# A new order for the instruction list of a fused attention and gated-MLP block

## The chip, the cores and the metric

The kernel runs on one core of one Trainium2 chip. The core has five engines that run on their own instruction streams: TensorE (PE, matrix products), VectorE (DVE), ScalarE (ACT), GpSimd (POOL) and SyncE (SP, which here issues DMAs). They wait for one another by semaphores. The metric is the device time of one execution in microseconds, as the median of three runs.

## The reference

One sequence of 2048 tokens with 448 features goes through two blocks whose normalized inputs are modulated by a conditioning vector `c`:

```
mod = silu(c) @ w_mod                      # six vectors: sa, ca, ga, sb, cb, gb
h = layernorm(x) * (1 + ca) + sa
q, k, v = split(h @ wqkv)                  # 16 heads of 28
p = softmax(q k^T / sqrt(28), masked to the last 256 positions)
x = x + ga * ((p v) @ wo)
h = layernorm(x) * (1 + cb) + sb
z = gelu(h @ w_in)                         # 1792 columns: z1 and z2, 896 each
g = w_sp @ layernorm(z2) + b_sp            # w_sp is 2048 x 2048
out = x + gb * ((z1 * g) @ w_out)
```

All data are bfloat16; products accumulate in float32.

## The kernel before

The tokens are cut into 16 tiles of 128, and four of these make a block `tb`. The program first collects a list of operations. Each has a number, the engines that could do it with a planned duration for each ("ways"), the operations it depends on, and the buffers it takes ("Hold", "Res"). Nothing in that list sets the order. The order is a text, `ORDER`: each entry is the number of an operation, one letter for the engine that does it (p TensorE, a ScalarE, v VectorE, g GpSimd, s SyncE), and the index of the buffer it takes. `Sched.order` reads the entries one after the other and appends each operation to its engine's stream; an engine does its stream strictly in that order. Buffers are given in list order too, so that who waits for whom over a buffer also follows from the list. `Sched.waits` then puts in the semaphore waits that the dependences need. The planned durations in the code only sort the waits of an instruction; they decide no order once `ORDER` stands.

The stages, with the lines that the prediction speaks of:

- The start. `w_mod`, `wqkv` and the first tokens are loaded. Statistics of a tile are taken on VectorE (L605, L608), then come the variance plus epsilon (L610, VectorE or GpSimd), its power of -1/2 (L613, GpSimd only), the negative scaled mean (L617 on VectorE, L620 on GpSimd), and the normalized tile (L625 on VectorE, L627 on ScalarE, L630 on GpSimd). Tiles are turned on TensorE (L692) and scaled into `hT` (L699, L701). The weights for q and k are copied into padded form `WQK` (L596, L597), and GpSimd and ScalarE clear `QBD` (L530, L531). Warm-up products (L561) keep TensorE running.
- Attention, for each tile and each half of the heads: scores into four PSUM banks (L952) and one bank more (L961), exponentials on ScalarE (L913), masks on VectorE (L968), the products with the values (L995). There is one set of four banks for the scores, so a new L952 can't begin before the exponential of the last one is read. Between these run the q, k and v projections of later blocks (L782, L811, L824) with their evictions (L792, L816, L817, L828, L829), the division (L1009, L1011), the output projection (L1019), the residual sum (L1024) and the second layer norm with the copy of its last columns (L633, L634). SyncE turns tiles by DMA; the result is scaled with the modulation (L682, L684 for the first norm, L1042 and L1044 for the second).
- The gated MLP. The z2 half (L1081, GELU L1092 and L1104 on ScalarE, squares L1113, small operations L1108, normalization L1096 on GpSimd, L1099 and L1118 on VectorE) and the z1 half (L1127, GELU L1135) are both products with half of TensorE's rows, written by the helper at L855 in groups of four steps that take two pairs of banks.
- The spatial products (L1151): 28 groups of 16 matmuls with 512 columns, which need all normalized z2 tiles and the transposed `w_sp` (wspA for the first two blocks, wspB for the others). VectorE adds the bias (L1155), GpSimd multiplies by z1 (L1158), TensorE makes the output product (L1170), VectorE adds the residual (L1181), SyncE stores.

## Time and profile before

| | us |
|---|---|
| three runs, median (lowest to highest) | 278.40 (278.39 to 279.79) |
| the profiled execution, its own time | 277.81 |
| its span, first to last instruction | 276.1 |
| TensorE busy with matmuls | 265.1 |
| VectorE busy | 161.2 |
| ScalarE busy | 134.8 |
| GpSimd busy | 124.2 |

The granted clock of TensorE is 1.0 throughout. "Busy" is the time in which an engine has an instruction under way; a matmul's end is modelled, so that a busy TensorE may still have waited a little. The span is about 1.7 us shorter than the profiled execution's time, since the time also holds what lies before the first and behind the last instruction. In a row of a group, the number after the bar is the busy time in all, then the mean duration of one in ns, then the idle time of the engine just before them with what ended it. In a row of the timeline stand the start and the duration in us. In a row of the stretches stand first the stretch, its length and the busy time of PE, PEld (weight loads), DVE, ACT and POOL with the number of instructions.

### The profile page before, as it was taken

The numbers are of one execution on the slowest core, as the hardware profiler recorded it, in microseconds if no ns is written. First come the engines' busy times: TensorE is split into PE (matmuls) and PEld (weight loads), VectorE is DVE, ScalarE is ACT, GpSimd is POOL, SyncE is SP. The second block draws the span as 40 slices with busy tenths as digits, with TensorE's granted clock in tenths as the row PEclk, the third lists the DMA queues.
The fourth block names the chain that finished last, engine by engine and source line by source line (L and its number), as shares of the span: only waits on it lengthen the run. The fifth ranks groups of instructions, "written<-read, shape, count | busy, mean of one in ns | idle before, by whom it ended". The sixth has DMA issues, their size and how long they took to land.

```text
span 276.1 us, 7474 instructions
## 1 busy us (share of the span) xinstructions
PE 265.1 (96%) x3230; PEld 142.0 (51%) x3230; DVE 161.2 (58%) x364; ACT 134.8 (49%) x185; POOL 124.2 (45%) x182
## 2 busy tenths in 40 slices
PE   5699999999999999999999799999999999999995
PEld 3465565557577565445444344444444444444453
DVE  6888998989899999985548101025040221322453
ACT  4589998899999998559997400000000000000000
POOL 7830528635107695786499300028370311543310
PEclk9999999999999999999999999999999999999999
DMA  7946955262333748545999999200000000001023
GB/s 216 304 167 198 255 104 106 41 96 60 69 71 57 106 67 172 104 92 103 184 183 212 161 203 190 49 0 0 0 4 0 0 17 2 0 17 33 19 86 97
DMA packets 67595, 26.54 MB, mean 96 GB/s; under 512 B 58021, under 2 KB 66474, under 8 KB 67562
## 3 DMA queue, kind: packets, MB, share of 16 engines
q1 hardware_dynamic: 67288, 25.61, 45.0%
q8 instruction: 25, 0.41, 0.6%
q10 hardware_dynamic: 274, 0.46, 0.5%
q14 instruction: 8, 0.07, 0.1%
HBM read 9.53 MB, written 1.84 MB: 41 GB/s over the span
## 4 chain that ended last, share of the span: by engine, by line
PE 77%; DVE 15%; ACT 2%; DMA 2%; issue 1%; POOL 1%; ACTq 0%; DVEq 0%
PE ps L1151 35%; PE ps L1081 8%; PE ps L1127 8%; PE ps L1170 8%; DVE PT L968 6%; PE ps L782 5%; PE ps L995 3%; PE ps L824 3%; PE ps L1019 3%; PE ps L952 2%; DMA wmod<-in_w_mod_dram 2%; DVE o_sb L1011 1%; DVE st_all L605 1%; DVE x_sb L1024 1%; POOL rs_all L613 1%
## 5 line engine op out<-in xcount | busy, mean ns | idle before, releaser
L913 ACT ACTIVATE PW<-ps 128x2048 bf16<-128x2048 f32 (+1 forms) x56 | 68.0, 1244 | 3.7 <-PE ps L952 2.1
L1155 DVE TENSOR_TENSOR tmpg<-ps,bsp_bc 128x512 bf16<-128x512 f32 x28 | 19.0, 690 | 80.9 <-PE ps L1151 66.4
L1158 POOL TENSOR_TENSOR z1T<-tmpg,z1T 128x512 bf16<-128x512 bf16 x28 | 31.7, 1152 | 76.1 <-DVE tmpg L1155 76.1
L1151 PE MATMUL ps<-wspA,z 128*128 128x512 bf16 x224 | 48.5, 380 | 1.7 <-ACT z1T L1135 1.7
L1151 PE MATMUL ps<-wspB,z 128*128 128x512 bf16 x224 | 49.2, 380 | 0.0
L968 DVE TENSOR_TENSOR PT<-PW,mask 128x1024 bf16<-128x1024 bf16 x56 | 37.9, 708 | 0.2 <-ACT PW L913 0.2
L1151 PEld LDWEIGHTS ps<-wspA,z 128*128 128x128 bf16 x224 | 21.8, 98 | 28.4 <-POOL z L1096 2.1
L1151 PEld LDWEIGHTS ps<-wspB,z 128*128 128x128 bf16 x224 | 21.9, 98 | 26.3
L613 POOL TENSOR_TENSOR rs_all<-ve_all,neghalf 128x1 f32<-128x1 f32 (+1 forms) x31 | 21.8, 710 | 14.3 <-DVE ve_all L610 13.2
L995 PE MATMUL ps<-Vaug,PT 128*128 128x32 bf16 x496 | 24.5, 177 | 0.8 <-DVE PT L968 0.4
L995 PEld LDWEIGHTS ps<-Vaug,PT 128*128 128x128 bf16 x496 | 21.5, 96 | 4.3 <-DVE PT L968 1.0
L1127 PE MATMUL ps<-hT,w_in 64*128 64x512 bf16 x196 | 22.1, 377 | 0.0
L1081 PE MATMUL ps<-w_in,hT 64*128 64x448 bf16 x224 | 22.1, 350 | 0.0
L1170 PE MATMUL ps<-w_out_g,z1T 128*128 128x448 bf16 (+2 forms) x126 | 22.0, 332 | 0.0
L995 PE MATMUL ps<-Vaug,PW 128*128 128x32 bf16 x224 | 20.4, 177 | 0.0
L782 PE MATMUL ps<-hT,WQK 128*128 128x512 bf16 x80 | 19.6, 380 | 0.1
L605 DVE BATCH_NORM_STATS2 st_all<-x_sb 128x6 f32<-128x448 bf16 x32 | 19.1, 610 | 0.1
L995 PEld LDWEIGHTS ps<-Vaug,PW 128*128 128x128 bf16 x224 | 17.7, 96 | 1.9
L1170 PEld LDWEIGHTS ps<-w_out_g,z1T 128*128 128x128 bf16 x126 | 11.7, 98 | 10.1
L630 POOL TENSOR_SCALAR xn<-x_sb,rs_all,ve_all 128x448 bf16<-128x448 bf16 x17 | 16.0, 944 | 1.1 <-DVE ve_all L617 0.5
L1135 ACT ACTIVATE z1T<-ps 128x512 bf16<-128x512 f32 x28 | 14.6, 604 | 3.4 <-PE ps L1127 3.3
L1081 PEld LDWEIGHTS ps<-w_in,hT 64*128 64x128 bf16 x224 | 10.8, 94 | 10.5 <-DVE mv_all L1108 0.3
(122 smaller groups left out, 356.0 us busy)
## 6 DMA issues: line engine op xcount, KB each, us to landing
out_dram<-fin SPq DMA_DIRECT2D x15, 112.0 KB, 1.7
x_sb<-in_A_x_dram SPq DMA_DIRECT2D x3, 448.0 KB, 4.5
wmod<-in_w_mod_dram SPq DMA_DIRECT2D x1, 1344.0 KB, 8.3
w_in<-in_B_w_in_dram SPq DMA_DIRECT2D x1, 1344.0 KB, 7.4
QBD<-qT SPq DMA_DIRECT2D x16, 64.0 KB, 2.1
w_out_g<-in_B_w_out_dram SPq DMA_DIRECT2D x1, 784.0 KB, 5.9
bsp_bc<-in_B_b_sp_dram SPq DMA_DIRECT2D x1, 512.0 KB, 5.2
x_sb<-in_A_x_dram SPq DMA_DIRECT2D x2, 224.0 KB, 3.6
```

The costliest lines, as they stand in the source:

```text
L605: st = [dve(0.62 if True else 0, lambda e, t=t, ci=ci, s=s: e.bn_stats(st_all[:, slot, t, ci, :], s()), deps(t), prio) for ci, s in enumer ...
L613: rs = pool(0.41 + 0.155 * len(tiles), lambda e: e.tensor_tensor(rs_all[:, slot, a:b], ve_all[:, slot, a:b], neghalf[:, 0:b - a], ALU.pow) ...
L782: m = pe(4 * MMS, [lambda e, h=h, g=g, kc=kc, tb=tb: e.matmul(ps[:, h.slot[0], :], lhsT=WQK[:, kc, 4 * g:4 * g + 4, :].rearrange("p a b -> ...
L913: ex = act(xdur, lambda e, out_ap=out_ap, in_ap=in_ap: e.activation(out_ap(), in_ap(), ACT.Exp, scale=SCALE), [s], v - 8.0 + u, takes, tab ...
L968: return dve(0.68, lambda e: e.tensor_tensor(cols(hp.slot[0] * 2048 + 1024 * k, [[256, 4], [128, 2], [1, 128]]), cols(at_w() + 128 + 192 * ...
L995: fns.append(lambda e, hp=hp, hO=hO, hi=hi, bi=bi, kb=kb, hd=hd, nb=nb, a=at[hi][bi], p_of=p_of: e.matmul(ps[:, hO.slot[0], 32 * hd:32 * h ...
L1081: return lambda e, kc, p0, start, stop: e.matmul(ps[:, hs[t % 2].slot[hf], 0:D], lhsT=hT[p0:p0 + 64, kc, t * 128:(t + 1) * 128], rhs=w_in[ ...
L1127: return lambda e, kc, p0, start, stop: e.matmul(ps[:, hs[b // 2].slot[b % 2], :], lhsT=w_in[p0:p0 + 64, kc, ft * 128:(ft + 1) * 128], rhs ...
L1151: m = pe(16 * MMS, [lambda e, h=h, si=si, ft=ft, tb=tb: e.matmul(ps[:, h.slot[0], :], lhsT=z2[:, si, ft * 128:(ft + 1) * 128], rhs=(wspA i ...
L1155: a = dve(0.7, lambda e, h=h, ht=ht, tb=tb: e.tensor_tensor(tmpg[:, ht.slot[0], :], ps[:, h.slot[0], :], bsp_bc[:, tb * 512:(tb + 1) * 512 ...
L1158: u = pool(1.16, lambda e, ht=ht, ft=ft, tb=tb: e.tensor_tensor(z1T[tb][:, ft, :], tmpg[:, ht.slot[0], :], z1T[tb][:, ft, :], ALU.mult), [ ...
L1170: return [lambda e, ft=ft: e.matmul(ps[:, h.slot[0], c0:c1], lhsT=z1T[t // 4][:, ft, (t % 4) * 128:(t % 4 + 1) * 128], rhs=w_out_g[:, ft, ...
```

## The change

The text `ORDER` is replaced by another with the same operations, two further warm-up products (76 and 77) aside. Nearly every entry stands in another place. 107 operations change engines as well: for instance, thirteen of the L617/L620 operations move from GpSimd to VectorE and three the other way, six normalized tiles move from GpSimd to VectorE and two the other way (L625, L630), and ScalarE has six hT scalings of the second norm (L1042) where it had one. In the code, four planned durations of GpSimd operations are raised; the instructions themselves stay as they are. An excerpt of the list, and all edits of the code:

```diff
@@ ORDER, the start @@
-2.a 25.v 35.g 0.s 26.v 27.v 28.v 38.g 39.g 3.a 4.s 36.g 45.a 33.g 29.v 5.s 30.v 31.v 37.g 32.v 40.g 6.s 7.s 41.g 138.v 139.v 140.v 141.g 46.p.0 48.a
...
-112.v 163.v 164.v 165.p.3 131.a 132.g 130.g 49.g 73.p.6 74.p.7 75.p.0 174.p.4.5 175.p.6.7 176.p 166.a 177.p 178.p 179.p 167.a 8.s 1.s 133.a 182.p
-180.p 183.p 181.p 150.v 151.v 152.g 153.g 9.s 10.s 11.s 134.a 188.p.0.1 189.p.2.3 14.s 13.s 12.s 16.s 15.s 156.v 157.v 158.v 159.g 154.v 136.v 155.v.2
-137.g 187.a 184.a 186.a 160.v 161.v.3 135.v 171.p.7 172.a 173.a 168.p.4 190.p 191.p 192.p 193.p 195.p 194.p 197.p 196.p 169.v 170.v 230.v 232.v
...
-224.p.6 213.p.7 210.p.0 383.a.0 388.p.0 217.a 225.a 389.a.1 228.p.7 214.a 229.a 34.g 52.g 51.g 239.g 42.g 223.v 240.v 243.v.0 244.g.1 44.g 43.g
...
+2.a 25.v 35.g 0.s 26.v 27.v 28.v 38.g 39.g 3.a 4.s 36.g 45.a 33.g 29.v 5.s 30.v 31.v 37.g 32.v 40.g 6.s 7.s 41.g 46.p.0 48.a 47.a 144.v 8.s 145.v 1.s
...
+14.s 71.p.0 72.p.3 165.p.2 112.v 111.v 162.p.3 12.s 131.v 130.a 166.v 133.g 163.v 16.s 167.a 73.p.6 74.p.7 75.p.0 76.p.6 174.p.4.5 150.v 164.a 13.s
+175.p.6.7 50.a 77.p.0 176.p 151.v 15.s 156.v 177.p 152.g 178.p 153.g 179.p 135.a 157.v 183.p 181.p 158.v 134.v 180.p 159.g 154.v 187.a 188.p.0.1 185.v
+189.p.2.3 155.a.2 136.g 190.p 160.v 191.p 161.v.3 42.g 168.p.7 171.p.5 137.g 192.p 169.v 193.p 49.g 194.p 172.v 182.p 170.a 197.p 195.p 196.p 173.v
+198.a 43.g 234.v 199.a 204.p.7 51.g 184.a 232.v 203.p.5 200.a 186.a 205.p.0 235.v 201.a 236.v 52.g 207.a 202.p.1 208.a 230.v 382.p.0 209.a 224.p.6
...
@@ ORDER, the end of attention @@
-817.p.0 818.p 772.p.1 820.a.3.2 822.a 823.v 824.v 847.a 547.g.0 849.g 548.g 744.v 773.v 687.v 518.g.2 825.p 850.g 826.p 914.p.0 519.g 827.v 828.v.0
-915.p.1 916.p 896.p.3 897.p.2 898.p 917.p 899.p 918.a 632.g 660.g 661.g 633.g 381.s 549.s 520.s 800.s 829.s 688.v 689.g 634.g.1 662.g 845.g 745.v
...
+546.v 716.v 800.s 817.p.0 547.g.1 772.p.1 577.g 548.v 744.v 822.a 896.p.0 823.v 897.p.1 816.v 578.s 773.v 898.p 824.v 818.p 825.p 549.s 717.v 629.v
...
@@ ORDER, the hand-over to the spatial products @@
-846.g 1032.a.1 945.a.0 999.g 1006.v 946.v 1033.g 913.v 1034.g 992.g 993.g 1027.v 1028.g 947.g 1000.v 1014.v 1007.v 1008.v 907.g 959.v 1035.v 977.g
...
-1053.p.0 1054.p 1085.p.3 1055.p 1086.p 1087.p 1009.g 1010.g 1011.g 994.v 1016.g 930.v 1017.g 1012.g 948.v 924.v 863.s 1057.a 1056.a 1091.a 1058.a
-1090.a 1059.a 1088.a 1089.a 894.s 895.s 882.s 886.s 887.s 890.s 893.s 891.s 892.s 880.s 883.s 1029.v 1018.v 1140.p.4 1110.p.5 1134.p.6 1135.v.0
...
+1085.p.3 1029.v 890.s 1064.a 1011.v 1012.g 1086.p 1065.a 1087.p 880.s 942.g 1052.p.2 1091.a 907.g 1090.a 1053.p.0 882.s 1054.p 977.g 881.s 1055.p
+845.g 1110.p.6 1059.a 883.s 840.g 1058.a 1057.a 1088.a 893.s 1089.a 1056.a 1140.p.7 894.s 886.s 887.s 1107.p.0 891.s 863.s 892.s 1104.p.1 884.s 895.s
...
@@ costs of GpSimd operations @@
-        ways = {"pool": (0.23, lambda e: e.tensor_scalar(ve_all[:, slot, a:b], mv_all[:, slot, a:b, 1], EPS, None, ALU.add))}
+        ways = {"pool": (0.31, lambda e: e.tensor_scalar(ve_all[:, slot, a:b], mv_all[:, slot, a:b, 1], EPS, None, ALU.add))}
-        return [rs, add({"dve": (0.16, by), "pool": (0.27, lambda e: e.tensor_scalar(ve_all[:, slot, a:b], mv_all[:, slot, a:b, 0], rs_all[:, slot, a:b], -1.0, ALU.mult, ALU.mult))}, [rs], prio)]
+        return [rs, add({"dve": (0.16, by), "pool": (0.33, lambda e: e.tensor_scalar(ve_all[:, slot, a:b], mv_all[:, slot, a:b, 0], rs_all[:, slot, a:b], -1.0, ALU.mult, ALU.mult))}, [rs], prio)]
-                         "pool": (0.25, lambda e: e.tensor_copy(to[:, h.slot[0], D:DP], to[:, h.slot[0], DP - 128:D]))}, [op], prio)]
+                         "pool": (0.28, lambda e: e.tensor_copy(to[:, h.slot[0], D:DP], to[:, h.slot[0], DP - 128:D]))}, [op], prio)]
-                return add({"dve": (0.13, fn), "pool": (0.2, fn)}, deps, v)
+                return add({"dve": (0.13, fn), "pool": (0.29, fn)}, deps, v)

```

## The prediction

> **What bounds the kernel now.** I read the page's head first, then the busy time of each engine in stretches cut at the first exponential, the last exponential and the two ends of the gated MLP. The columns behind each stretch are its length, then the busy time of TensorE's matmuls, its weight loads, VectorE, ScalarE and GpSimd.

> ```profile
> span 276.1 us, 7474 instructions
> ...
> 0.00:18.75 18.75, 13.72 (x129) 8.74 (x130) 14.86 (x44) 11.63 (x26) 12.35 (x26) 1.00 0.81 243
> ...
> 24.00:107.40 83.40, 82.09 (x1993) 52.32 (x1990) 79.17 (x173) 79.41 (x83) 41.62 (x54) 1.00 0.53 98
> ...
> 109.20:153.50 44.30, 44.28 (x430) 20.90 (x428) 31.25 (x89) 33.74 (x63) 33.22 (x66) 1.00 0.83 152
> 153.50:155.20 1.70, 0.04 (x1) 0.07 (x2) 1.29 (x1) 1.68 (x4) 1.16 (x2) 1.00 1.18 57
> 155.20:273.20 118.00, 118.00 (x574) 55.34 (x574) 28.19 (x44) 1.37 (x3) 32.66 (x29) 1.00 0.20 46
> ```

> From 155.2 to 273.2 TensorE never stops (118.00 of 118.00), and from 109.2 to 153.5 it has 0.02 us idle: no order can shorten these two stretches, since the change adds and removes no matmul there. What is left is the start (18.75 us to the first exponential), the attention stretch, where ScalarE is idle for 83.40 - 79.41 = 4.0 us and VectorE for 4.2 us, and one hole of 1.7 us at 153.5. That is all a new order can win; it can lose without such a bound, in the attention stretch above all.

> **The change part by part.** Comparing the two lists entry by entry: both hold the same operations but for two more warm-up matmuls (76 and 77) at the start. Every engine's order changes. VectorE goes from 364 to 380 entries, GpSimd from 178 to 157, ScalarE from 168 to 173. The four raised GpSimd costs change no instruction; they only move the planned times.

> *The start.* These are VectorE's, GpSimd's and ScalarE's instructions there (start, duration).

> ```profile
> 7.69 0.86 DVE L701 TENSOR_SCALAR hT<-ps,modT 128x256 bf16<-128x256 bf16 x2 [0.45 <-PE ps L692]
> ...
> 10.50 0.27 DVE L596 COPY WQK<-wq_st 128x448 bf16<-128x448 bf16 x1
> 10.69 0.38 DVE L625 TENSOR_SCALAR xn<-x_sb,mv_all,rs_all 128x448 bf16<-128x448 bf16 x1
> 11.54 1.17 DVE L625 TENSOR_SCALAR xn<-x_sb,mv_all,rs_all 128x448 bf16<-128x448 bf16 x1
> 12.63 1.10 DVE L596 COPY WQK<-wq_st 128x448 bf16<-128x448 bf16 x1
> ...
> 10.88 0.61 POOL L597 COPY WQK<-wq_st 128x448 bf16<-128x448 bf16 x1
> 11.63 1.97 POOL L531 MEMSET QBD<- 128x1024 f32 x2
> ...
> 7.74 0.58 ACT L596 ACTIVATE WQK<-wq_st 128x448 bf16<-128x448 bf16 x1 [1.29 <-DMA wq_st<-in_A_wqkv_dram]
> 18.75 1.02 ACT L913 ACTIVATE PT<-ps 128x1024 bf16<-128x1024 f32 x1
> ```

> The same normalization takes 0.38 us at 10.69 and 1.17 at 11.54, the same copy 0.27 at 10.50 and 1.10 at 12.63; during the long ones GpSimd clears QBD (two memsets, 1.97 us). Both long ones stand on the way to the first exponential: 0.79 + 0.83 = 1.6 us. The new list puts these copies (134, 135, 136) ahead of the normalization, gives tile 2's normalization (155) to ScalarE, and moves the two memsets (51, 52) behind. Two things take some of it back. The weight copy 131 moves from ScalarE to VectorE ahead of the two L701, and its data comes only at 7.74, so those start 7.74 + 0.27 - 7.69 = 0.3 us late, and tile 2's statistics behind them. And GpSimd still runs a 0.61 us copy (136) where normalization 161 comes, which can hold it for up to that. I take -1.0 us; the ends are -1.6 (nothing given back) and 0 (all of it, by a chain now hidden).

> [...]

> *The attention stretch.* Rows by group within 24.0 to 107.4 (count | busy us, mean ns), one instruction from the timeline, two waits; the second L968 row is of 70 to 80 us, where GpSimd does nothing (count: shortest/median/longest).

> ```profile
> L816 ACT ACTIVATE KT<-ps 128x512 bf16<-128x512 f32 x1 | 0.6, 592 | 0.0
> L767 ACT ACTIVATE KT<-ps 128x256 bf16<-128x256 f32 x1 | 0.4, 378 | 0.0
> ...
> 107.42 0.80 ACT L1042 ACTIVATE hT<-hT,modT 128x512 bf16<-128x512 bf16 x1
> ...
> ACT PW L913 <- PE ps L952: 2.1, 7, 0.5
> ...
> L968 DVE TENSOR_TENSOR PT<-PW,mask 128x1024 bf16<-128x1024 bf16 x54 | 36.7, 709 | 0.2 <-ACT PW L913 0.2
> L605 DVE BATCH_NORM_STATS2 st_all<-x_sb 128x6 f32<-128x448 bf16 x18 | 10.8, 610 | 0.0
> ...
> L1024 DVE TENSOR_TENSOR x_sb<-ps,x_sb 128x448 bf16<-128x448 f32 x12 | 7.4, 617 | 0.7 <-PE ps L1019 0.6
> ...
> L817 DVE CAST KT<-ps 128x512 bf16<-128x512 f32 x3 | 2.0, 675 | 0.0
> L617 DVE SCALAR_TENSOR_TENSOR ve_all<-mv_all,rs_all 128x4 f32<-128x4 f32 (+1 forms) x4 | 1.5, 377 | 0.8 <-POOL rs_all L613 0.7
> L625 DVE TENSOR_SCALAR xn<-x_sb,mv_all,rs_all 128x448 bf16<-128x448 bf16 x3 | 1.4, 471 | 0.0
> ...
> L684 DVE TENSOR_SCALAR hT<-hT,modT 128x512 bf16<-128x512 bf16 x3 | 1.1, 394 | 0.0
> L574 DVE COPY gg_sb<-ps 128x448 f32<-128x448 f32 x1 | 0.6, 619 | 0.0
> ...
> L968 DVE TENSOR_TENSOR PT<-PW,mask x5: 659/684/687, 74.0 to 77.6; 128x1024 bf16<-128x1024 bf16 x5
> ...
> L630 POOL TENSOR_SCALAR xn<-x_sb,rs_all,ve_all 128x448 bf16<-128x448 bf16 x13 | 13.0, 1003 | 0.7 <-DVE ve_all L617 0.3
> ...
> L620 POOL TENSOR_SCALAR ve_all<-mv_all,rs_all 128x1 f32<-128x1 f32 x6 | 3.7, 623 | 0.5
> ...
> DVE ve_all L617 <- POOL rs_all L613: 1.7, 4, 0.7
> ```

> ScalarE, between its first and its last exponential: two more K evictions (L816, 2 x 0.59), one more hT scaling (0.80), the gate copy from VectorE (L574; 0.62, no ScalarE row, bounds 0.38 and 0.80 from its other copies), two L767 fewer (2 x 0.38). Sum +1.8 us on an engine with 4.0 us idle, of which 2.1 us are waits for the scores (L952).

> VectorE, between its first and last mask: statistics 13 to 9 (-4 x 0.61), L817 three to one (-2 x 0.68), residual sums 12 to 14 (+2 x 0.62), norms +3 x 0.47, hT scalings +2 x 0.39, L617 +3 x 0.38; the others cancel. Sum: -2.44 - 1.35 + 1.23 + 1.41 + 0.79 + 1.13 = +0.8 us.

> GpSimd up to the last mask: four L620 fewer (-4 x 0.62) and one L630 (-1.0); the rest, scalings and small copies that come and go, stays within 0.4 us: about -3.5 of 41.6 us. A mask takes 709 ns on average against 684 with GpSimd silent: 54 x 0.025 = 1.35 us lost to it in the stretch, of which 3.5/41.6 is 0.1 us. That relief is small.

> TensorE: three of the four steps of the first MLP group (896 to 898, L855) move ahead of the last three attention products. That work fills the wait for the last exponentials, and TensorE's idle in the stretch is 83.40 - 82.09 = 1.3 us.

> So the stretch gets +1.8 us on ScalarE, and must eat 1.8 of its 4.0 us idle to stay as long. Ends: +1.8 (idle unchanged) and -2.2 (no idle left). The list cannot tell which; I take the middle, 0. GpSimd's work moved onto VectorE is hidden only while VectorE keeps its remaining idle of 4.2 - 0.8 = 3.4 us.

> *After attention.* ScalarE gets four more hT scalings (4 x 0.80 = 3.2 us) between 107 and 153, where it is idle 44.30 - 33.74 = 10.6 us: hidden. Then the hole:

> ```profile
> 153.53 3.04 ACT L1135 ACTIVATE z1T<-ps 128x512 bf16<-128x512 f32 x6 [1.72 <-PE ps L1127]
> 153.57 1.09 POOL L1096 TENSOR_SCALAR z<-z,rs_all,ve_all 128x896 bf16<-128x896 bf16 x1
> ...
> 155.16 2.10 PE L1151 MATMUL ps<-wspA,z 128*128 128x512 bf16 x9 [1.68 <-ACT z1T L1135]
> ```

> The first spatial product waits for a free bank (ScalarE's GELU) and for the last normalized tile (GpSimd, done at 154.66). In the new list it takes a bank of the group before the last (1110 in bank 6, freed by GELU 1090), so the first cause goes. Next late is GpSimd, whose four normalizations (1012, 942, 907, 977) now come in a row, the last beside TensorE's last two steps. I take -1.0; ends -1.7 and +0.5 (half a normalization more than now).

> *The last stretch.* Its order changes most, but only a stall could cost.

> ```profile
> L1155 DVE TENSOR_TENSOR tmpg<-ps,bsp_bc 128x512 bf16<-128x512 f32 x28 | 19.0, 690 | 80.9 <-PE ps L1151 66.4
> L1158 POOL TENSOR_TENSOR z1T<-tmpg,z1T 128x512 bf16<-128x512 bf16 x28 | 31.7, 1152 | 76.1 <-DVE tmpg L1155 76.1
> L1151 PE MATMUL ps<-wspA,z 128*128 128x512 bf16 x224 | 48.5, 380 | 1.7 <-ACT z1T L1135 1.7
> ...
> L1170 PE MATMUL ps<-w_out_g,z1T 128*128 128x448 bf16 (+2 forms) x126 | 22.0, 332 | 0.0
> ...
> bsp_bc<-in_B_b_sp_dram SPq DMA_DIRECT2D x1, 512.0 KB, 5.2
> ...
> 148.50 24.03 SPq L477 DMA_TRANSPOSE wspB<-in_B_w_sp_dram  x16
> ```

> On SyncE the bias load moves behind 13 of the 16 wspB transposes: 148.5 + 13 x 1.50 + 5.2 = 173. A group takes 16 x 48.5/224 = 3.46 us and there are eight banks, so the ninth needs one at 155.2 + 27.7 = 182.9: hidden by 10 us, minus one eviction. At the end two output groups (2 x 7 x 22.0/126 = 2.4 us) instead of four cover the last L1155 and L1158 (0.69 + 1.15 = 1.84 us): hidden, with 0.6 us to spare. Term 0.

> Sum: -1.0 + 0 - 1.0 + 0 = -2.0 us. The profiled execution took 277.81 us, so 275.8; the median of the runs, 278.40, lies 0.6 above it, so **276.4** is what I predict for the median.

> **The rivals.** *A, VectorE stuck behind GpSimd (slower).* L617 on VectorE waits for GpSimd's power (L613), and all queued behind it, masks included, waits too. Up to the last mask there are 12 such entries instead of 8 and 11 norms on VectorE instead of 9. At the longest wait (0.7) and the longest hold (1.17 - 0.38), 4 x 0.7 + 2 x 0.79 = 4.4 us: 276.4 + 4.4 = 280.8. It makes the kernel slower by over 0.5% from 3.4 us up. For it: VectorE has only 4.2 us idle in 83. Against: four such waits are 1.7 us now, and most moved entries come late. *B, ScalarE's stream is the wall (no change).* Its idle stays: +1.8, so 278.2. For it: the waits for scores are a turn-around through one set of banks (L952 writes where the exponential before reads), which an order hardly shortens. Against: it has 4.0 us. *C, all holes close (faster).* -1.6, -1.3 (TensorE's attention idle), -1.7: 4.6 us, 273.8. [...]

> **How the numbers follow.** Half a per cent, 1.4 us, is about what a measurement of this kernel can tell from no change. My forecast 0.41, C 0.12: faster 0.53. B 0.22: same. A 0.25: slower. The range reaches to A's and C's prices: 273.5 to 281.0; the forecast's own is 274.5 to 277.8.

> **What would show it.** Start: the first exponential at about 17.7, no L625 or L596 over 0.7 us before it. Attention: first to last exponential still 89 us; ScalarE's waits for L952 under 2.1 us. Hole: first L1151 within 0.7 us of the last L1127. End: matmuls back to back for 118 us. I am wrong if VectorE's waits for L613 grow past 3 us, if a mask waits behind them, or if the stretch between the exponentials grows by more than 2 us.

## The result and the profile after

The new list takes 275.25 us (median; 274.60 to 276.79), the old one beside it 278.72 us (278.08 to 279.79): a ratio of 0.9874, with an interval of [0.984, 0.9908], that is 3.5 us or 1.3% less. The profiled execution of the new kernel took 275.39 us with a span of 273.7; that of the old one had 277.81 and 276.1. So the pair of profiles that is compared below holds 2.4 of the 3.5 us; the other 1.1 us is what these two executions differ from the medians by. Here and below a median is of all executions, while a ratio is taken on those within 1.5% of the fastest of their kernel, without two of e3 and three of e4, and is no quotient of medians.

The columns of the next fence are those of the prediction's stretches: length, then busy time of TensorE, weight loads, VectorE, ScalarE and GpSimd. It is the new kernel, cut at the first exponential, the last exponential and the first spatial product, and at the last stretch.

```profile
0.00:19.81 19.81, 15.83 (x133) 9.97 (x134) 13.75 (x45) 10.99 (x25) 13.21 (x30) 1.00 0.75 230
...
152.74:270.74 118.00, 118.00 (x574) 55.49 (x574) 27.99 (x44) 3.04 (x6) 36.75 (x33) 1.00 0.25 49
...
19.81:107.65 87.84, 87.22 (x2068) 56.11 (x2068) 82.04 (x189) 85.75 (x92) 30.47 (x45) 1.00 0.52 103
107.65:152.74 45.09, 45.09 (x461) 21.46 (x457) 31.34 (x102) 38.11 (x68) 25.80 (x55) 1.00 0.83 155
```

The same two middle stretches of the old kernel, from the last exponential on up to its first spatial product:

```profile
18.75:107.52 88.77, 87.36 (x2071) 55.74 (x2070) 83.52 (x184) 84.75 (x91) 43.35 (x59) 1.00 0.53 102
107.52:155.16 47.64, 45.96 (x466) 22.14 (x463) 34.22 (x92) 37.04 (x68) 35.81 (x69) 1.00 0.85 153
```

Stage by stage, in us (the first exponential stands for its start, the last for its end):

| stage | old | new | difference | predicted |
|---|---|---|---|---|
| start, to the first exponential | 18.75 | 19.81 | +1.06 | -1.0 |
| attention, first to last exponential | 88.77 | 87.84 | -0.93 | 0 |
| hand-over, last exponential to first spatial product | 47.64 | 45.09 | -2.55 | -1.0 |
| the rest | 120.92 | 120.94 | +0.02 | 0 |

In attention ScalarE works 1.0 us more (84.75 to 85.75) and is idle 1.9 us less (88.77 - 84.75 = 4.02 us before, 87.84 - 85.75 = 2.09 after). In the hand-over TensorE had 47.64 - 45.96 = 1.68 us idle and now has none; besides it has 0.87 us less to do there (45.96 to 45.09): four matmuls of the output projection (L1019, 8 in this stretch instead of 12) and the first 0.57 us of the gated MLP (L1081, begun at 107.08) now run before the last exponential ends at 107.65. How the hole closed stands in the timeline of the new kernel (start, duration):

```profile
149.45 3.23 POOL L1096 TENSOR_SCALAR z<-z,rs_all,ve_all 128x896 bf16<-128x896 bf16 x3
...
149.76 2.97 PE L1127 MATMUL ps<-hT,w_in 64*128 64x512 bf16 x26
...
152.74 4.49 PE L1151 MATMUL ps<-wspA,z 128*128 128x512 bf16 x20
```

GpSimd's normalizations end at 152.68, the last L1127 at 152.73, and the first spatial product begins at 152.74. In the old kernel the last GpSimd normalization ran from 153.57 to 154.66.

### The profile page after: what moved, and what is told of

The parts are those of the page before. It is cut to its first block, busy times and chain, and to the rows that moved or that the text cites. A ratio compares the mean times of both kernels' runs of the same rounds, so it can differ in the third digit from the quotient of the medians.

```text
span 273.7 us, 7480 instructions
## 1 busy us (share of the span) xinstructions
PE 266.2 (97%) x3232; PEld 143.0 (52%) x3232; DVE 155.6 (57%) x380; ACT 137.9 (50%) x190; POOL 106.2 (39%) x161
## 3 DMA queue, kind: packets, MB, share of 16 engines
HBM read 9.53 MB, written 1.84 MB: 42 GB/s over the span
## 4 chain that ended last, share of the span: by engine, by line
PE 89%; ACT 7%; DMA 2%; DVE 1%; issue 1%; SPq 0%; DVEq 0%
PE ps L1151 35%; PE ps L1081 8%; PE ps L1127 8%; PE ps L1170 8%; PE ps L782 6%; PE ps L995 6%; PE ps L952 4%; ACT PW L913 4%; PE ps L1019 4%; PE ps L824 3%; PE ps L961 2%; DMA wmod<-in_w_mod_dram 2%; PE ps L811 1%; PE ps L561 1%; PE ps L740 1%; ACT qT L767 1%
## 5 line engine op out<-in xcount | busy, mean ns | idle before, releaser
L913 ACT ACTIVATE PW<-ps 128x2048 bf16<-128x2048 f32 (+1 forms) x56 | 67.9, 1255 | 1.8 <-PE ps L952 0.7
L1155 DVE TENSOR_TENSOR tmpg<-ps,bsp_bc 128x512 bf16<-128x512 f32 x28 | 19.0, 689 | 85.6 <-PE ps L1151 74.0
L1158 POOL TENSOR_TENSOR z1T<-tmpg,z1T 128x512 bf16<-128x512 bf16 x28 | 31.9, 1151 | 75.3 <-DVE tmpg L1155 75.3
L1151 PE MATMUL ps<-wspB,z 128*128 128x512 bf16 x224 | 49.5, 379 | 0.0
L1151 PE MATMUL ps<-wspA,z 128*128 128x512 bf16 x224 | 49.0, 379 | 0.0
L968 DVE TENSOR_TENSOR PT<-PW,mask 128x1024 bf16<-128x1024 bf16 x56 | 36.6, 681 | 0.7 <-ACT PW L913 0.7
L1151 PEld LDWEIGHTS ps<-wspA,z 128*128 128x128 bf16 x224 | 21.9, 98 | 26.7 <-POOL z L1096 0.5
L1151 PEld LDWEIGHTS ps<-wspB,z 128*128 128x128 bf16 x224 | 21.9, 98 | 26.3
L613 POOL TENSOR_TENSOR rs_all<-ve_all,neghalf 128x1 f32<-128x1 f32 (+1 forms) x31 | 20.6, 674 | 35.1 <-DVE ve_all L610 33.8
L995 PE MATMUL ps<-Vaug,PT 128*128 128x32 bf16 x496 | 23.9, 177 | 0.0
L1170 PE MATMUL ps<-w_out_g,z1T 128*128 128x448 bf16 (+2 forms) x126 | 21.9, 332 | 0.0
L1081 PE MATMUL ps<-w_in,hT 64*128 64x448 bf16 x224 | 21.9, 349 | 0.0
L1127 PE MATMUL ps<-hT,w_in 64*128 64x512 bf16 x196 | 21.8, 376 | 0.0
L605 DVE BATCH_NORM_STATS2 st_all<-x_sb 128x6 f32<-128x448 bf16 x32 | 18.9, 610 | 0.0
L1170 PEld LDWEIGHTS ps<-w_out_g,z1T 128*128 128x128 bf16 x126 | 11.7, 98 | 10.0
L1135 ACT ACTIVATE z1T<-ps 128x512 bf16<-128x512 f32 x28 | 14.3, 609 | 4.5 <-PE ps L1127 4.5
L1081 PEld LDWEIGHTS ps<-w_in,hT 64*128 64x128 bf16 x224 | 10.7, 94 | 10.6 <-ACT PW L913 0.4
L952 PE MATMUL ps<-qT,KT 32*128 32x64 bf16 (+2 forms) x1008 | 15.3, 198 | 0.3 <-ACT PW L913 0.2
## 6 DMA issues: line engine op xcount, KB each, us to landing
bsp_bc<-in_B_b_sp_dram SPq DMA_DIRECT2D x1, 512.0 KB, 5.4
```

The costliest lines, as they stand in the source:

```text
L613: rs = pool(0.41 + 0.155 * len(tiles), lambda e: e.tensor_tensor(rs_all[:, slot, a:b], ve_all[:, slot, a:b], neghalf[:, 0:b - a], ALU.pow) ...
L913: ex = act(xdur, lambda e, out_ap=out_ap, in_ap=in_ap: e.activation(out_ap(), in_ap(), ACT.Exp, scale=SCALE), [s], v - 8.0 + u, takes, tab ...
L952: fm.append(lambda e, hm=hm, k=k, qi=qi, key=key, kn=kn, lo=lo, hi=hi, col=col, p0=p0, t=t, j=j: e.matmul(ps[p0:p0 + kn, hm.slot[t], k * 1 ...
L968: return dve(0.68, lambda e: e.tensor_tensor(cols(hp.slot[0] * 2048 + 1024 * k, [[256, 4], [128, 2], [1, 128]]), cols(at_w() + 128 + 192 * ...
L995: fns.append(lambda e, hp=hp, hO=hO, hi=hi, bi=bi, kb=kb, hd=hd, nb=nb, a=at[hi][bi], p_of=p_of: e.matmul(ps[:, hO.slot[0], 32 * hd:32 * h ...
L1081: return lambda e, kc, p0, start, stop: e.matmul(ps[:, hs[t % 2].slot[hf], 0:D], lhsT=hT[p0:p0 + 64, kc, t * 128:(t + 1) * 128], rhs=w_in[ ...
```

## The experiments

Twelve kernels ran. This table has their medians, the ratio to the old kernel beside them on the same chip, the three stages from their profiles (us), and the time from which TensorE's granted clock was full, as the trace has it on record (the old kernel: 5.05, the new one: 10.59; two traces have no such record). "Old" and "new" name parts of the two lists; in the fifth to the eleventh the edits are a few entries.

| run | list | median (runs) | ratio [interval] | first exponential | attention | hand-over | clock full from |
|---|---|---|---|---|---|---|---|
| e1 | old start, then new | 273.84 (5) | 0.984 [0.9809, 0.9871] | 17.91 | 87.83 | 45.10 | 10.62 |
| e2 | old to the last exponential, then new | 279.91 (12) | 1.0052 [1.0021, 1.0084] | 17.38 | 88.79 | 48.80 | none |
| e3 | new, three MLP steps put back | 278.04 (12) | 0.9965 [0.9939, 0.999] | 17.50 | 87.92 | 48.86 | 5.90 |
| e4 | new, engines of VectorE/GpSimd put back | 277.36 (12) | 0.9926 [0.989, 0.9962] | 19.21 | 87.91 | 45.99 | none |
| e5 | new, two warm-ups behind the w_mod wait | 275.65 (7) | 0.9901 [0.9866, 0.9937] | 20.16 | 87.83 | 45.35 | 11.56 |
| e6 | old, the same | 278.82 (12) | 1.0018 [0.9995, 1.0041] | 20.45 | 88.89 | 47.76 | 10.10 |
| e7 | e1, the same | 274.31 (6) | 0.9859 [0.9828, 0.9891] | 18.94 | 87.83 | 45.35 | 10.45 |
| e8 | e5, a QBD clear later | 275.27 (10) | 0.9909 [0.9875, 0.9943] | 19.20 | 87.84 | 45.31 | 9.88 |
| e9 | new, one eviction later | 274.48 (4) | 0.9857 [0.9841, 0.9872] | 19.16 | 87.83 | 45.12 | 11.30 |
| e10 | new, two warm-ups in the w_mod wait | 274.30 (6) | 0.9852 [0.9824, 0.988] | 20.09 | 87.83 | 45.12 | 11.50 |
| e11 | e9 and e10 | 274.69 (5) | 0.9859 [0.9838, 0.988] | 17.64 | 87.83 | 45.13 | 6.45 |
| e12 | new to the last exponential, then old | 280.53 (8) | 1.0073 [1.0049, 1.0097] | 17.23 | 87.83 | 50.85 | 5.32 |

The rest, from the first spatial product on, took 120.7 to 120.94 us in all of them. In the traces of e1 to e4 the kernel's lines stand one higher than in the others (L692 is L693 there).

### The start exchanged (e1)

The list begins with the old entries up to the first score product (382); every entry that is not yet listed follows in the new order, without 76 and 77.

```diff
@@ ORDER @@
-2.a 25.v 35.g 0.s
...
-52.g 207.a 202.p.1 208.a 230.v 382.p.0
+2.a 25.v 35.g 0.s
...
+200.a 201.a 204.p.4 208.a 203.p.7 207.a 205.p.0 209.a 382.p.0
```

> The list of before up to the first scores (operation 382), then the new list for all that is left; the two further warm-up products are left out. In the two traces the first exponential starts at 18.75 us before and at 19.81 after. Theory (the new order of the start itself is worse, and the gain was made later): the first exponential comes back to 18.8, and the kernel gets 1.0 us faster than after, 1.7% faster than before (ratio 0.983). Rival (the late start of that one execution is chance, a late load, and the start's order is worth nothing or the forecast gain): no faster than after, ratio to before 0.987 or above, up to 0.991 if the forecast gain of 1.0 us was there in the other executions.

Measured: 273.84 us, 0.984 [0.9809, 0.9871]; the first exponential comes at 17.91 us instead of 19.81, attention and hand-over are those of the new list (87.83 and 45.10). So the gain does not come from the new start, and the profile suggests that the new start is worse; the two compare well, since the clock was full from 10.62 and 10.59 us. The medians cannot prove that: the interval overlaps that of the new list, [0.984, 0.9908]. And e1's start is not the old kernel's in every entry: the cut puts GpSimd's mask (42, 43) ahead of the two clears of QBD (51, 52), which then ran at 12.73 us, when VectorE's normalization and weight copy (0.53 and 0.26 us) were over.

### Attention and hand-over crossed (e2, e12)

e2 takes the old entries up to the last exponential and then what is not yet listed in the new order, without 76 and 77; e12 takes the new entries up to the last exponential and then what is not yet listed in the old order. Which list each part comes from:

```diff
@@ ORDER, from the first entry to the last exponential: e2 @@
-new
+old
@@ ORDER, behind the last exponential: e12 @@
-new
+old
```

> The list of before up to the last exponential (operation 822), then the new list. From the end of the last exponential to the first spatial product the traces show 47.6 us before and 45.1 after. Theory (the larger part of the gain is in the hand-over: the hole of 1.7 us and the first-layer steps that fill the wait for the last exponentials): 2.0 to 2.5 us faster than before, ratio 0.992, first spatial product about 45.1 us behind the last exponential. Rival (the hand-over is short only because attention in the new order leaves less work behind): under 1.2 us faster, ratio 0.996 or above, hole still there.

> The new list up to the last exponential, the old order from there on. It separates the attention term from the hand-over: attention 87.8 to 87.9 us as in the new kernel. Theory that the hand-over's gain of 2.5 us stands in the list behind attention: the hole of 1.7 us before the first spatial product is back and the time from the last exponential to that product is 47.0 to 47.7 us, ratio 0.994 to 0.997. Rival, that the gain comes from what the new attention order has finished early: 45 to 46 us and a ratio of 0.987 to 0.991. The last stretch 120.9 us by both.

The length of attention goes with the list that attention is in: 88.77 us (old kernel), 88.79 (e2) and 88.89 (e6) with the old order, 87.83 to 87.92 in the nine kernels with the new. ScalarE's waits for scores between 24.0 and 107.5 us, in us, times, longest, for the new kernel (in e12 also 0.7 in two):

```profile
ACT PW L913 <- PE ps L952: 0.7, 2, 0.5
```

Against 2.1 us in 7 waits in the old kernel (and the same in e2), the new order leaves 0.7 us in two, and with it goes the -0.93: the gain there is the order's, whatever follows.

The hand-over behaves otherwise. Each order fits its own attention (47.64 and 45.09) and both crosses are worse than either: 48.80 in e2, 50.85 in e12. Both crosses are slower than the old kernel. Neither theory held for either: e2 has no hole, but 48.80 us where 45.1 were expected; for e12 47.0 to 47.7 us were expected by the one and 45 to 46 by the other. Why they were wrong in e12 shows in two stretches, in its group of the first spatial product, in a wait of TensorE, and in two rows of VectorE:

```profile
104.31:107.72 3.41, 0.78 (x18) 0.47 (x17) 3.38 (x10) 2.00 (x3) 0.78 (x2) 1.00 0.96 251
107.72:111.13 3.41, 3.30 (x38) 1.73 (x39) 2.90 (x7) 0.00 (x0) 2.26 (x6) 0.50 0.65 99
```

```profile
L1151 PE MATMUL ps<-wspA,z 128*128 128x512 bf16 x6 | 1.5, 378 | 1.5 <-POOL z L1096 1.5
```

```profile
PE ps L995 <- DVE ve_all L610: 2.4, 1, 2.4
```

```profile
104.91 1.14 DVE L605 BATCH_NORM_STATS2 st_all<-x_sb 128x6 f32<-128x448 bf16 x2
...
106.24 0.66 DVE L968 TENSOR_TENSOR PT<-PW,mask 128x1024 bf16<-128x1024 bf16 x1
```

The hole before the first spatial product is back (1.5 us, behind GpSimd's normalization). In addition TensorE waits 2.4 us before its last products with the values. The last masks come late, because the seam, where the two lists are joined, puts four statistics (two L605, two L608), which the old list has ahead of the last exponential, in front of them in VectorE's stream; and the old order has nothing to put on TensorE meanwhile (its MLP steps stand behind these products). Then the granted clock is down to 0.50 for 3.41 us. In the old kernel the same work ran at full clock (1.00 from 108 to 116 us).

In e2 TensorE waits for masks (2.0 us) and for the transposed attention output (0.7 us); the MLP steps themselves wait for nothing there:

```profile
PE ps L996 <- DVE PT L969: 2.0, 2, 1.3
PE ps L1020 <- DMA hT<-o_sb: 0.7, 1, 0.7
```

```profile
109.70 0.18 DVE L634 COPY xn<-xn 128x64 bf16<-128x64 bf16 x1 [2.83 <-POOL xn L631]
...
110.33 0.68 DVE L969 TENSOR_TENSOR PT<-PW,mask 128x1024 bf16<-128x1024 bf16 x1
```

Here too the seam puts entries in front of the masks on VectorE, those that the new list has ahead of the last exponential; one is a copy that waits 2.83 us for GpSimd's normalization. So the hole goes with the list behind attention (back in e12, gone in e2); for the rest of the hand-over's gain the crosses show only what a seam costs.

### The three MLP steps put back (e3)

```diff
@@ ORDER, the end of attention @@
-822.a 896.p.0 823.v 897.p.1 816.v 578.s 773.v 898.p 824.v 818.p 825.p
+822.a 823.v 816.v 578.s 773.v 824.v 818.p 825.p
...
-826.p 899.p
+826.p 896.p.0 897.p.1 898.p 899.p
```

> The new list with one thing undone: the three steps of the first MLP group (896, 897, 898) stand behind the last attention product (826) again. Theory (they fill TensorE's wait for the last exponentials, worth what is left of the 2.5 us when the hole of 1.7 is taken off): 0.8 us slower than after, ratio to before 0.990, with an idle or stalled TensorE between the last scores and the last value products. Rival (TensorE has other work or is no limit there): same as after within 0.3 us.

Attention stays at 87.92 us, the hand-over grows by 3.77 us to 48.86, and the ratio from 0.9874 to 0.9965. Two stretches of e3, one group of TensorE between 105 and 118 us, and the first MLP group:

```profile
104.89:108.30 3.41, 1.32 (x38) 1.14 (x40) 3.41 (x8) 1.81 (x2) 0.00 (x0) 1.00 0.98 267
108.30:111.72 3.42, 3.42 (x20) 1.39 (x18) 3.27 (x11) 0.00 (x0) 2.89 (x6) 0.50 0.64 122
```

```profile
L996 PE MATMUL ps<-Vaug,PT 128*128 128x32 bf16 x24 | 1.2, 177 | 2.1 <-DVE PT L969 2.1
```

```profile
108.14 7.16 PE L1082 MATMUL ps<-w_in,hT 64*128 64x448 bf16 x56
```

The first MLP group of the old kernel, then of the new one, where its first part stands ahead of the last value products:

```profile
109.16 5.47 PE L1081 MATMUL ps<-w_in,hT 64*128 64x448 bf16 x56
```

```profile
107.08 2.25 PE L1081 MATMUL ps<-w_in,hT 64*128 64x448 bf16 x22
...
110.36 3.39 PE L1081 MATMUL ps<-w_in,hT 64*128 64x448 bf16 x34
```

Without the steps TensorE stands for 2.1 us in two waits (1.7 and 0.4) before its last value products, waiting for masks, and then runs 3.42 us at a granted clock of 0.50. So the steps are worth the wait that they fill and, on top, a drop of the clock that follows it. Of the 3.77 us, 48.86 - 47.30 = 1.56 are idle time behind the last exponential, by the stretch from 105.42 to 154.28:

```profile
105.42:154.28 48.86, 47.30 (x464) 22.36 (x465) 31.90 (x102) 38.12 (x69) 25.76 (x55) 0.97 0.81 145
```

The other 47.30 - 45.09 = 2.21 us are longer busy time: 7.16 - 5.47 = 1.69 for the same matmuls at the lower clock, and the rest, about the 0.57 us that the steps run ahead of the last exponential's end in the new kernel. The drop is no accident of one execution: one stretch of 3.42 us at half clock takes 0.006 off the mean granted clock of some 275 us, and that mean is 0.993 or 0.994 in all twelve executions of e3 and 0.988 (two such stretches) to 0.994 in e12's eight; of the new list's six it is 0.999 or 1.0 in five. A wait alone does not bring the drop each time: e2's profile, with waits of 0.7, 1.3 and 0.7 us, has none (its clock reads 1.00 from 106 to 116 us, and its MLP matmuls average 349 ns, as in the new kernel), but the mean is 0.988 to 0.994 in five of its twelve executions, and these are its five slowest (280.65 to 281.59 us).

In the traces of e12 and e3 the granted clock is 0.50 for 3.41 and 3.42 us, and TensorE had been busy for 0.78 and 1.32 us of the 3.41 us just before.

### VectorE's and GpSimd's operations on their old engines (e4)

The sequence is the new one; the 54 operations numbered 244 and up that had gone from GpSimd to VectorE or back are on their old engine again. Three of them:

```diff
@@ ORDER @@
-344.v.3
+344.g.3
...
-403.v
+403.g
...
-605.v.2
+605.g.2
```

> The new list with every entry in its place, but the 54 operations from number 244 on that changed between VectorE and GpSimd are done by the engine of before again (L610, L617/L620, L625/L630, L633/L634, L684, L1044, L1108). Rival to the order itself (what pays is GpSimd's work taken off, since the two engines hold each other up: GpSimd was busy for 43.4 us of the attention stretch before and 31.5 after): attention and the hand-over lose at least 1.5 us, ratio 0.993 or above. Theory (the order of the streams pays, ScalarE's idle of 4.0 going to 2.1 us; VectorE was busy for 83.5 us of the 88.8 before and 82.6 after, and has room): within 0.6 us of after, ratio 0.986 to 0.990.

Attention keeps its length, 87.91 us, although GpSimd works 39.89 us in it instead of 30.47 and the masks take 705 ns on average again instead of 681 (the old kernel had 709). Stretch and masks of e4, then the masks of the new kernel:

```profile
19.21:107.12 87.91, 87.30 (x2068) 56.08 (x2068) 82.05 (x177) 85.77 (x92) 39.89 (x57) 1.00 0.50 102
```

```profile
L969 DVE TENSOR_TENSOR PT<-PW,mask 128x1024 bf16<-128x1024 bf16 x54 | 36.6, 705 | 1.1 <-ACT PW L914 1.0
```

```profile
L968 DVE TENSOR_TENSOR PT<-PW,mask 128x1024 bf16<-128x1024 bf16 x54 | 35.3, 681 | 0.7 <-ACT PW L913 0.7
```

So the faster masks, and GpSimd's relief as a whole, are not what made attention shorter; the sequence is. The engine moves count behind it: the hand-over is 0.9 us longer, 0.8 of it a wait of TensorE between 105 and 153 us for a scaling on VectorE:

```profile
PE ps L1082 <- DVE hT L1045: 0.8, 1, 0.8
```

Neither expectation held to the number: attention and hand-over together lose 0.97 us, where one theory allowed 0.6 and the other asked for 1.5. The times of e4 spread from 274.45 to 279.09 us; which part of the kernel that spread sits in was not traced.

### What the start lost (e5 to e8)

In the profile of the new kernel TensorE is slow around 8 us: the first eight turns of tiles (L692) take 1.06 us, in the old kernel's 0.61. These four kernels were to find out whether TensorE's standing still for w_mod does it, with two more warm-up products, and whether the clear of QBD (operation 49, a memset on GpSimd) holds tile 3's normalization.

```diff
@@ ORDER, e5: new; e6: old; e7: e1 @@
-55.p
+55.p 63.p.2 64.p.3
@@ ORDER, e8: e5, and @@
-161.v.3 42.g 168.p.7 171.p.5 137.g 192.p 169.v 193.p 49.g
+161.v.3 49.g 42.g 168.p.7 171.p.5 137.g 192.p 169.v 193.p
```

> The new list with two more warm-up products (63 and 64) between the first and the second modulation product (55 and 56), where TensorE waits 1.0 us for the weights. In six traces so far the eight transposes L692 that follow take either 0.61 us (first exponential at 17.4 to 18.8, once with the new start, 17.5) or 1.06 us (17.9 to 19.8, once with the old start). Theory (chance decides whether TensorE has come to full speed by then, and that wait is what it hangs on): with the wait filled L692 takes 0.61 us, the first exponential comes by 18.2, and the kernel is 0.5 to 1.5 us faster than after, ratio to before 0.982 to 0.986. Rival (the new start's order itself is late): L692 still 1.06 us or first exponential still at 19 or later, ratio 0.987.

> The list of before with the same two warm-up products at the same place. Theory (chance of the start, same in both lists): first exponential by 18.8 in every case, L692 0.61 us, median 0.3 to 1.0 us lower than before, ratio 0.997 or a little less, the rest as in the trace of before (88.8 us of attention, hole of 1.7 us). Rival (the products only delay the second modulation product): same as before or up to 0.4 us slower.

> The start of before (up to operation 382), then the new list, with the two warm-up products. With TensorE at full speed in both, this against the new list with the same two products shows what the order of the start is worth by itself. Theory (nothing, within 0.5 us): ratio to before within 0.002 of the new list with warm-up products. Rival 1 (my forecast, the new start is worth 1.0 us): 0.003 to 0.004 higher. Rival 2 (the new start costs, as the first two traces show): 0.003 to 0.004 lower.

> The new list with the two warm-up products, and GpSimd's first clearing of QBD (49) behind the normalization of tile 3 (161). In the trace of after that normalization (L625 at 13.28) takes 0.97 us where the free one takes 0.40, while GpSimd clears from 13.17 to 14.12. Theory (the two engines hold each other up, and this hold stands on the way to the first exponential): L625 of tile 3 takes about 0.4 us, the first exponential comes 0.5 us earlier than in the new list with warm-up products, ratio 0.002 lower. Rival (GpSimd's copy of the weights, 137, then holds it, or other work bounds the first exponential): no difference.

The edit missed its aim by one entry. The wait for w_mod stands before operation 55, so the products came behind the wait and only put off the first turns. TensorE in e5:

```profile
6.19 0.59 PE L540 MATMUL ps<-sc_sb,wmod 128*128 128x1 bf16 x16 [0.85 <-DMA wmod<-in_w_mod_dram]
...
8.51 1.06 PE L692 MATMUL ps<-ident,xn 128*128 128x128 bf16 x8
```

TensorE was slow in all four (1.06 us), so nothing on its pace follows from the edit. Of the four starts the old entries (e7: first exponential at 18.94 us) are 1.2 us ahead of the new (e5: 20.16); the medians, 274.31 and 275.65, are 1.3 us apart. Up to 0.55 us of the 1.2 is the clock, full 1.11 us earlier in e7 (an estimate: half of 1.11, since in the old kernel warm-up products start 0.42 us apart before its clock is full and 0.22 after), and e7 has the later clears of e1. In e8 the first exponential came 0.96 us earlier than in e5, but nothing shows that the later clear did it: w_mod landed 0.45 us earlier, and the clock was full 1.68 us earlier, worth up to 0.84 by the same estimate; tile 3's normalization still took 0.92 us in it, and its median of 275.27 is not distinguishable from 275.65.

e6 showed something else. It has the old kernel's start, and here tile 3's normalization took 2.06 us, with both memsets of QBD beside it (GpSimd, second fence):

```profile
12.93 2.06 DVE L625 TENSOR_SCALAR xn<-x_sb,mv_all,rs_all 128x448 bf16<-128x448 bf16 x1
```

```profile
13.02 1.83 POOL L531 MEMSET QBD<- 128x1024 f32 x2
```

In the old kernel's own profile the same instruction took 1.17 us. And in e2, with the same entries up to there, it took 0.40 and the weight copy 0.27:

```profile
11.52 0.40 DVE L626 TENSOR_SCALAR xn<-x_sb,mv_all,rs_all 128x448 bf16<-128x448 bf16 x1
11.83 0.27 DVE L597 COPY WQK<-wq_st 128x448 bf16<-128x448 bf16 x1
```

```profile
12.47 1.84 POOL L532 MEMSET QBD<- 128x1024 f32 x2 [0.81 <-DMA x_sb<-in_A_x_dram]
```

There GpSimd waited 0.81 us for a transfer of x, so that its memsets came after VectorE was through, and the first exponential stands at 17.38 us instead of 18.75. The hold of 0.8 + 0.8 us that the old profile shows is thus a meeting that the list allows and the arrival of a DMA decides.

### One eviction and the wait for w_mod (e9, e10, e11)

In the new kernel VectorE's stream before the second pair of tiles, and TensorE's beside it, read:

```profile
12.61 0.42 DVE L768 CAST qT<-ps 128x256 bf16<-128x256 f32 x1 [0.99 <-PE ps L740]
12.95 0.29 DVE L617 SCALAR_TENSOR_TENSOR ve_all<-mv_all,rs_all 128x1 f32<-128x1 f32 x1
13.28 0.97 DVE L625 TENSOR_SCALAR xn<-x_sb,mv_all,rs_all 128x448 bf16<-128x448 bf16 x1
```

```profile
8.16 1.06 PE L692 MATMUL ps<-ident,xn 128*128 128x128 bf16 x8
...
11.32 2.24 PE L740 MATMUL ps<-hT,WQK 128*128 128x256 bf16 x19
14.31 0.62 PE L692 MATMUL ps<-ident,xn 128*128 128x128 bf16 x8 [0.75 <-DVE xn L625]
```

Operation 185, an eviction of q (L768), went from ScalarE to VectorE and stands ahead of tile 3's L617. It waits 0.99 us for TensorE, with L617 and L625 queued behind it.

```diff
@@ ORDER, e9 (and e11) @@
-187.a 188.p.0.1 185.v 189.p.2.3 155.a.2 136.g 190.p 160.v 191.p 161.v.3
+187.a 188.p.0.1 189.p.2.3 155.a.2 136.g 190.p 160.v 191.p 161.v.3 185.v
@@ ORDER, e10 (and e11) @@
-62.p.7 54.p.1
+62.p.7 54.p.1 63.p.2 64.p.3
```

> The new list with one entry moved: VectorE's eviction of q for the first two tiles (operation 185, L768) comes behind tile 3's normalization (161, L625) instead of ahead of the small L617 (160) that feeds it. Theory: the new start is late because VectorE stands 1.0 us at this L768, waiting for TensorE's L740, while tile 3's L617 and L625 are queued behind it with their data ready. Then L617 runs about 0.9 to 1.0 us earlier, L625 begins 1.0 to 1.2 us earlier with respect to the second L701, the first exponential comes at 18.6 to 18.9 us where TensorE's first eight L692 take 1.06 us (at 18.2 or before where they take 0.61), and the median is 0.983 to 0.986 of the kernel before. Rival, GpSimd's memsets of QBD alone hold the start up: L625 still takes over 0.9 us or the wait moves to L701, the first exponential stays at 19.2 or later, and the ratio stays at 0.987 to 0.990. Attention 87.8 to 87.9 us and the time from the last exponential to the first spatial product 45.1 us by both.

> The new list with two more warm-up products (63 and 64, L561) directly behind the first group of conditioning products (54), that is, in TensorE's wait of about 1 us for the second part of w_mod, which the earlier try missed by one entry. Theory: TensorE is slow after that wait in some executions because it stood still in it. Then the first eight L692 take 0.61 us instead of 1.06, the two L561 ahead of them 0.59 instead of 1.01, and the first exponential comes 0.8 to 0.9 us earlier than in the new kernel's profile (19.81), at about 18.9; the ratio to the kernel before is 0.984. Rival: the pace of the start falls one way or the other by chance whatever TensorE does there: the L692 take 1.06 us again, or the ratio stays at 0.987 to 0.990. The rest as in the new kernel.

> The new list with the eviction 185 behind tile 3's normalization and the two warm-up products in the wait for w_mod. If both theories hold the gains add up: first exponential at 17.7 to 18.1 us, span 271.6 to 272.0, ratio to the kernel before 0.979 to 0.982, below the 0.984 of the kernel with the old start and the new rest. If only the eviction counts, the ratio is 0.983 to 0.986.

e9, VectorE and TensorE:

```profile
11.32 0.49 DVE L617 SCALAR_TENSOR_TENSOR ve_all<-mv_all,rs_all 128x1 f32<-128x1 f32 x1 [0.38 <-POOL rs_all L613]
11.84 0.40 DVE L625 TENSOR_SCALAR xn<-x_sb,mv_all,rs_all 128x448 bf16<-128x448 bf16 x1
```

```profile
7.48 1.06 PE L692 MATMUL ps<-ident,xn 128*128 128x128 bf16 x8
...
11.32 2.24 PE L740 MATMUL ps<-hT,WQK 128*128 128x256 bf16 x19
13.68 0.61 PE L692 MATMUL ps<-ident,xn 128*128 128x128 bf16 x8
```

L625 starts 1.44 us earlier, but the turns that wait for it start only 0.63 us earlier, and the first exponential 0.65 (19.81 to 19.16): from 12.24 on TensorE itself is late, with a row of projections (L740) that in both profiles begins at 11.32 and ends at 13.56. The expected 18.6 to 18.9 us was missed for that reason: e9's first turns were 0.68 us earlier than the new kernel's, but its clock was full 0.71 us later (11.30 instead of 10.59). The median, 274.48 us, lies 0.8 below the new list's, within the uncertainty of both.

What else made TensorE late shows against e1, whose old start began its first turns at the same slow pace and the same time (7.49 us):

```profile
9.62 2.84 PE L741 MATMUL ps<-hT,WQK 128*128 128x256 bf16 x20
12.50 0.62 PE L693 MATMUL ps<-ident,xn 128*128 128x128 bf16 x8
```

From the first turns to the second it takes 12.50 - 7.49 = 5.0 us, in e9 13.68 - 7.48 = 6.2. The new list has three things more in between: the added warm-up products 76 and 77 and two projections (190, 191) that the old one had behind the turns. The first warm-up puts the first L740 from 9.62 to 10.04; the second stands between two L740 and takes about as much (0.42 us from its start at 10.90 to the next L740); some 0.3 us are left for the two projections. All of that ran at half speed, and e9 ran so for 0.68 us longer than e1 (until 11.30 instead of 10.62), which makes 0.34 of the 1.2 us; the entries themselves then come to about 0.85 us of TensorE at full clock. That is an estimate from two traces: no kernel left out 76 and 77 alone.

e10 and e11 give TensorE the same two products in the same wait, and came out apart (first fence e10, second e11):

```profile
6.77 1.00 PE L540 MATMUL ps<-sc_sb,wmod 128*128 128x1 bf16 x24 [0.41 <-DMA wmod<-in_w_mod_dram]
8.44 1.06 PE L692 MATMUL ps<-ident,xn 128*128 128x128 bf16 x8
```

```profile
6.32 0.77 PE L540 MATMUL ps<-sc_sb,wmod 128*128 128x1 bf16 x24
7.38 0.61 PE L692 MATMUL ps<-ident,xn 128*128 128x128 bf16 x8
```

In e10 w_mod came late and a wait of 0.41 us was left over: the slow pace. In e11 none was left: the quick pace, and the first exponential stands at 17.64 us with a span of 271.5, as expected of both edits together. Yet the old kernel and e3 had the quick pace too after a wait of 0.74 and 0.62 us, without any filling, and e1 the slow one after 0.51; and e11's four executions beside the profiled one took 1.0 to 1.8 us longer than its 273.26, so that its ratio is 0.9859 and not the expected 0.979 to 0.982. So no run shows that filling the wait brings the quick pace dependably.

What the pace is, the traces have on record: the time of the first change of the granted clock, in the last column of the table. Up to that time TensorE runs at half speed. In the old kernel, with the clock full from 5.05 us, six warm-up products from 2.40 us on take 2.74 us, the last 0.63, so that they start (2.74 - 0.63) / 5 = 0.42 us apart; three from 7.71 on take 0.81, the last 0.38, and start (0.81 - 0.38) / 2 = 0.22 us apart. In the new kernel, with the clock full from 10.59 us, a warm-up product takes 634 ns between 9.4 and 9.8 us and 379 between 11.0 and 11.4:

```profile
L561 PE MATMUL ps<-ident 128*128 128x512 bf16 x2 | 1.1, 634 | 0.0
```

```profile
L561 PE MATMUL ps<-ident 128*128 128x512 bf16 x1 | 0.4, 379 | 0.0
```

In four traces on record the clock is full from 5.05 to 6.45 us on, in the eight others from 9.88 to 11.56; 9.88 - 6.45 = 3.43. All later changes stand a whole number of 3.413 us from the first: in e3 (108.30 - 5.90) / 30 = 3.413 to the drop and 3.42 to its end, in e12 (107.72 - 5.32) / 30 = 3.413 to the drop, in the new kernel (273.42 - 10.59) / 77 = 3.413 to a change at the end. So the changes of these three traces lie on a grid of 3.413 us, and where the grid lies against the first instruction differs between executions. In the four traces with the early clock the first change, at 5.05 to 6.45 us, comes as the first warm-up products end or soon after (they run from 2.4 to 5.1 us in the old and the new kernel). If the grid holds for the eight others too, it has a step at 6.47 to 8.15 us in them (an estimate: 3.41 off the time on record), with the wait for w_mod in the 3.41 us before it, and the clock was not full until the next. No run shows why.

With an early clock the new start is as good as the old: 17.50 (e3), 17.23 (e12) and 17.64 (e11) with the new entries, 17.38 (e2) and 18.75 (the old kernel, with its hold) with the old. With a late one it is behind: 19.81 (the new kernel) and 19.21 (e4) against 17.91 (e1).

In the medians e1, e9, e10 and e11 (0.984 to 0.9859) lie a little below the new list (0.9874), with intervals that overlap; none is shown to beat it.

## Why the prediction was right, and where its steps failed

The direction was right and the time lay within the range, 275.25 us against 276.4 predicted. The sum was not: 3.5 us were gained and 2.0 forecast, and three of its four terms were off. In the profiles their errors, +2.06, -0.93 and -1.55, cancel to -0.4; that they do is luck.

**The start: predicted -1.0 (ends -1.6 and 0), measured +1.06 in the two profiles.** Part of the +1.06 is chance of the two executions, whose clock was full from 5.05 and from 10.59 us. With an early clock the new entries do what was forecast: e3 and e12 have the first exponential at 17.50 and 17.23 and tile 3's L625 at 0.40 us. The failing step is "Both long ones stand on the way to the first exponential: 0.79 + 0.83 = 1.6 us", taken as a price of the old list. The rows were right for that execution; but the same entries gave 0.40 and 0.27 us and a first exponential at 17.38 in e2, and 2.06 us for the normalization in e6. And two things were not in the sum: what the new entries put on TensorE ahead of the second pair of tiles (76 and 77 were named but not costed; 190 and 191 not seen; about 0.85 us at full clock by the estimate above, twice that at half), and the eviction 185 queued ahead of tile 3's L617 (0.65 us at the first exponential, with the hold that it leads into). With a late clock the new start does not shed the hold either: in the new kernel's profile tile 3's L625 took 0.97 us at 13.28, beside a memset. The hold that the prediction did reserve 0.61 us for, by GpSimd's weight copy, was not seen: in e9 such a copy (11.99, 0.66) ran beside L625 (11.84), which took 0.40. For the medians the other three terms give -0.93 - 2.55 + 0.02 = -3.46 of the measured -3.47, so that there the start comes to about nothing. This is a remainder, not a measurement. e1 and e7 speak for a small loss, but against an old start whose clears come later.

**Attention: predicted 0 (ends -2.2 and +1.8), measured -0.93.** The mechanism was the named one, more work on ScalarE against less idle time. The busy time was mis-sized: it grew by 1.0 us, not 1.8. The four items are all there, but in the trace they add only 1.6: a row begins some 0.1 us before the one ahead of it ends (L828 at 101.28, with the exponential from 99.50 running 1.88), so its duration is more than it adds. And the 62 exponentials cover 0.5 us less, 71.4 instead of 71.9, as more of them follow without a gap. The idle time fell by 1.9 us, which is about the 1.8 taken, so that it more than paid for the smaller addition: the waits for scores went from seven to two. Rival B's claim on the turn-around through one set of banks, "which an order hardly shortens", is refuted. The relief from GpSimd was put at 0.1 us; the masks went from 709 to 681 ns, 54 x 0.028 = 1.5 us of VectorE's time. It bought nothing (e4), so leaving it out of the sum was right for the wrong reason.

**The hand-over: predicted -1.0 (ends -1.7 and +0.5), measured -2.55.** The hole closed fully, -1.68: both causes went, and GpSimd's four normalizations end 0.05 us before TensorE's last step. The mis-sized term is the three MLP steps, costed at nothing because TensorE's idle in attention was small. With four matmuls of the output projection they take 0.87 us out of the hand-over, and putting them back costs 3.77 us (e3), of which the prediction had no part: the wait they fill is longer with the new order (2.1 us) than with the old, where the waits for masks between 103 and 118 us are 0.4 in all, and the clock falls to 0.50 for 3.42 us behind it.

**The last stretch: predicted 0, measured +0.02,** with matmuls back to back for 118.00 of 118.00 us.

**The rivals.** A did not come: VectorE's waits for L613 up to the last mask are 0.6 us in two, less than the 1.7 us before.

```profile
DVE ve_all L617 <- POOL rs_all L613: 0.6, 2, 0.3
```

B is out by the waits for scores. C was right on the hole and on much of attention's idle TensorE time (87.22 of 87.84 us busy, against 87.36 of 88.77), wrong on the start.

## What to carry to other kernels

A long row beside another engine's memset is the price of a meeting in one execution (0.40, 1.17 and 2.06 us for one normalization behind the same entries); before it goes into a sum as the price of an order, look whether a DMA's arrival decides the meeting. When a list is rewritten, the entries in front of the first critical wait count on every engine, added "free" warm-up products and evictions moved to another engine included. Work that fills a TensorE wait of some two microseconds is to be costed with the clock that TensorE can lose behind an unfilled one (in e3 0.50 for 3.42 us, behind waits of 2.1); and two halves of a list that each win in their own surroundings can both lose when crossed, by what the seam leaves ahead of the critical entries. Two profiles of a start are compared only when the clock was full from the same time in both (here from 5.05 us at the earliest and 11.56 at the latest).
